# Strassen's seven products of quarters in place of eight, in the second product of an RWKV-6 plus SiLU kernel

**Chip, cores, metric.** One core of a Trainium2 chip. The metric is the device time of one execution in microseconds (us); lower is better.

## The reference

An attention block with a decayed state is followed by a two-layer feed-forward block over its output. Only the last part changes.

```python
# attention: r, k, v, w of shape (4 batches, 8 heads, 768 steps, 48); y has the same shape
for t in range(S):
    y[:, :, t] = r_t . (state + (u * k_t) v_t);  state = w_t * state + k_t v_t      # condensed
# feed-forward: x = y as (3072 tokens, 384)
h = x @ w_in                       # (3072, 384) @ (384, 2048)
g = h * (1.0 / (1.0 + np.exp(-h)))
out = g @ w_out                    # (3072, 2048) @ (2048, 384)  <- "the second product"
```

All arithmetic is fp32; w_in and w_out come as float64 and are rounded on the chip in the first 130 us.

## The kernel before

The 3072 tokens are taken in 12 units of 128 time steps x 2 batches. A unit's attention part (`mix`) has a serial chain of seven levels: TensorE makes score products (`p_sc`), VectorE copies them under a mask and multiplies r, and only then can the next level's products start. Between these steps the program puts independent feed-forward work of earlier units, so that TensorE always has something to do: the second product of the unit two back (`downs`), then the first product of the unit one back (`ups`).

```python
def up(i, m):                                     # first product, 2 of 16 feature blocks
    p_h = ps.tile([128, 2, TU], F32, name="p_h", bufs=2)
    # ... 6 matmuls of 256 columns ...
    nc.scalar.activation(out=gt[i, m], in_=p_h, func=AF.Silu)

def down(i, b, part, parts=4):                    # second product of batch b, 4 of 16 feature blocks
    if part == 0:
        po[i, b] = ps.tile([128, DM], F32, name="p_o", bufs=2)
    for f in range(part * FC // parts, (part + 1) * FC // parts):
        nc.tensor.matmul(po[i, b], lhsT=gt[i, f // 2][:, f % 2, b * L:(b + 1) * L], rhs=w_out_sb[:, f, :],
                         start=(f == 0), stop=(f == FC - 1))
    if part == parts - 1:
        ob = pt.tile([128, DM], F32, name="ob")
        nc.vector.tensor_copy(out=ob, in_=po[i, b])
        # ... store ...

def merge(*lists):                                # each list has shares; steps are ordered by their middle
    # ...
for i in range(3, NU):
    merge((mix(i), 0.0, 1.0), (downs(i - 2) + ups(i - 1), 0.0, 1.0))
merge((downs(NU - 2) + ups(NU - 1) + downs(NU - 1), 0.0, 1.0))
```

The order of steps is the order of each engine's queue. PSUM is the memory that TensorE's results land in, SBUF the one that holds the other tiles. Each tile in PSUM (`ps.tile`, at most 512 fp32 columns here) has a bank of its own; the program keeps eight of them (two each for `p_m`, `p_sc`, `p_h`, `p_o`).

## Time and profile before

| | before |
|---|---|
| time, median of the first 4 runs | 795.12 us (794.55 to 798.07) |
| TensorE busy | 93% of the span |
| units 5 to 11, level 0 to level 0 | 60.07 us |
| tail after the last attention step | 728.20 to 793.8 us |

First the engines' work in one unit, from one level 0 to the next (columns: stretch in us, its length, then per engine busy us and instructions):

```profile
core 0: us, PE busy (x) PEld busy (x) DVE busy (x) ACT busy (x) POOL busy (x), PEclk, DMA share, GB/s
259.02:319.09 60.07, 59.41 (x351) 45.25 (x351) 24.59 (x39) 9.64 (x20) 20.32 (x29) 1.00 0.33 52
```

TensorE (PE) has 0.66 us free out of 60.07. VectorE (DVE) works 24.59 us. Second, TensorE where the attention part of a unit ends (columns: start us, length us, engine, line, operation, out<-in, shapes, count, in brackets the idle time before and what ended it):

```profile
712.98 1.04 PE L368 MATMUL p_m<-ident,tk 128*128 128x128 f32 x8
714.30 1.13 PE L382 MATMUL p_m<-state,tr 128*128 128x96 f32 x8 [0.29 <-ACT kq L370]
```

L368 turns k back; L382 begins y of the first batch in the PSUM buffer that ScalarE (ACT) still has to empty. This is one of the few places where TensorE waits at all.

### The profile page before, as it was taken

The page shows a single profiled execution, that of the slowest core. Times are in us where ns is not written, and L with a number is a line of the kernel's source. Part 1 is how long each engine was busy: PE and PEld are TensorE (multiplying, and loading weights), DVE is VectorE, ACT ScalarE, POOL GpSimd, SP SyncE. Part 2 cuts the span into 40 slices and gives each one's busy share as a digit, 9 for nine tenths or more (in the row PEclk, how much of TensorE's full clock was granted, in tenths as well). Part 3 has the DMA queues.
Part 4 walks back from the last instruction along what each step waited for, and adds up shares of the span by engine and source line. Part 5 has one row for each costly group of instructions (what it writes and reads, how often), then busy time and mean ns, then how long its engine had stood idle before and what let it go on. Part 6 is the DMA issues. An engine that isn't in the chain of part 4 may idle for free.

```text
span 793.8 us, 11597 instructions
## 1 busy us (share of the span) xinstructions
PE 739.6 (93%) x4232; PEld 565.2 (71%) x4232; DVE 324.3 (41%) x489; ACT 161.8 (20%) x300; POOL 283.8 (36%) x398
## 2 busy tenths in 40 slices
PE   4486689999999999999999999999999999999998
PEld 3375577687688688688588588588588588588684
DVE  3675785431443443443443443443443442440000
ACT  3236345112121021021021021022012012021020
POOL 8555765521531531522522522522432431520000
PEclk9976799999999999999999999999999999999999
DMA  9986053022232522522522522422422120000000
GB/s 197 269 178 192 1 117 53 19 32 25 55 64 26 86 45 26 96 34 25 96 35 26 94 36 38 78 34 26 91 35 26 42 50 1 10 11 1 21 1 20
DMA packets 215880, 45.82 MB, mean 58 GB/s; under 512 B 207504, under 2 KB 210704, under 8 KB 215824
## 3 DMA queue, kind: packets, MB, share of 16 engines
q1 hardware_dynamic: 215680, 44.89, 30.4%
q8 instruction: 34, 0.56, 0.3%
q10 hardware_dynamic: 144, 0.20, 0.1%
q14 instruction: 22, 0.18, 0.1%
HBM read 40.30 MB, written 4.72 MB: 57 GB/s over the span
## 4 chain that ended last, share of the span: by engine, by line
PE 82%; POOL 6%; issue 5%; DVE 4%; ACT 2%; DVEq 0%; POOLq 0%
PE p_h L466 31%; PE p_o L476 29%; PE p_sc L331 11%; PE p_m L386 5%; PE p_m L382 3%; PE p_m L397 2%; POOL tk L362 2%; DVE tr L346 1%; DVE score L340 1%; POOL tw L293 1%; POOL w_in_sb L194 1%; ACT gt L469 1%; PE p_m L418 1%; PE p_m L277 1%; ACT kq L370 1%
## 5 line engine op out<-in xcount | busy, mean ns | idle before, releaser
L466 PE MATMUL p_h<-xt,w_in_sb 128*128 128x256 f32 x1152 | 272.6, 390 | 0.0
L476 PE MATMUL p_o<-w_out_sb,gt 128*128 128x384 f32 x768 | 258.6, 490 | 0.0
L466 PEld LDWEIGHTS p_h<-xt,w_in_sb 128*128 128x128 f32 x1152 | 216.6, 193 | 32.6 <-issue 0.2
L340 DVE COPY_PREDICATED score<-mask,p_sc 128x512 f32<-128x512 int8 x168 | 138.4, 888 | 221.5 <-PE p_sc L331 219.6
L476 PEld LDWEIGHTS p_o<-w_out_sb,gt 128*128 128x128 f32 x768 | 142.3, 190 | 93.6
L362 POOL TENSOR_TENSOR tk<-tk,tw 128x256 f32<-128x256 f32 x168 | 120.5, 741 | 124.0 <-PE p_sc L331 56.4
L331 PEld LDWEIGHTS p_sc<-tr,tk 48*128 48x128 f32 x1344 | 88.8, 199 | 69.7 <-issue 30.8
L331 PE MATMUL p_sc<-tr,tk 48*128 48x128 f32 x1344 | 105.3, 299 | 33.5 <-DVE tr L346 21.1
L469 ACT ACTIVATE gt<-p_h 128x512 f32<-128x512 f32 x96 | 57.3, 597 | 355.6 <-PE p_h L466 355.6
L322 ACT COPY tk<-tk 128x256 f32<-128x256 f32 x72 | 32.4, 450 | 178.3 <-POOL tk L362 133.1
L293 POOL TENSOR_TENSOR tw<-tw 128x512 f32<-128x512 f32 (+6 forms) x84 | 37.5, 446 | 86.8 <-DVE tw L268 65.1
L346 DVE TENSOR_TENSOR tr<-tr,tw 128x512 f32<-128x512 f32 x84 | 67.4, 803 | 0.0
L401 POOL TENSOR_TENSOR state<-state,tw 128x384 f32<-128x384 f32 x16 | 13.2, 826 | 120.1 <-PE p_m L382 120.1
L480 DVE COPY ob<-p_o 128x384 f32<-128x384 f32 x24 | 13.4, 556 | 96.8 <-PE p_o L476 96.8
L389 DVE TENSOR_TENSOR xb<-p_m,ydiag 128x384 f32<-128x384 f32 x24 | 13.4, 557 | 75.7 <-PE p_m L386 75.7
L308 POOL TENSOR_TENSOR ydiag<-vt,diag 128x384 f32<-128x384 f32 x24 | 19.9, 828 | 64.8 <-DVE diag L305 61.4
L407 DVE TENSOR_TENSOR state<-p_m,state 48x192 f32<-48x192 f32 x32 | 11.4, 355 | 48.2 <-PE p_m L397 48.0
L277 PE MATMUL p_m<-ident,raw 128*128 128x128 f32 x96 | 18.1, 338 | 12.7 <-DMA raw<-in_w_dram 5.9
L277 PEld LDWEIGHTS p_m<-ident,raw 128*128 128x128 f32 x96 | 14.0, 174 | 16.9 <-POOL mask L235 5.8
L301 POOL TENSOR_TENSOR ruk<-ruk,u_bc 128x384 f32<-128x384 f32 x24 | 24.0, 1000 | 1.9
L386 PE MATMUL p_m<-vq,score 128*128 128x48 f32 x192 | 24.6, 284 | 0.0
L382 PE MATMUL p_m<-state,tr 128*128 128x96 f32 x160 | 21.8, 279 | 2.9 <-ACT kq L370 2.9
(55 smaller groups left out, 437.2 us busy)
## 6 DMA issues: line engine op xcount, KB each, us to landing
vt<-in_v_dram SPq DMA_DIRECT2D x24, 192.0 KB, 3.7
out_dram<-ob SPq DMA_DIRECT2D x24, 192.0 KB, 1.9
w_out_sb<-in_moe_w_in_dram SPq DMA_DIRECT2D x5, 768.0 KB, 6.8
w_out_sb<-in_moe_w_out_dram SPq DMA_DIRECT2D x4, 768.0 KB, 5.2
own<-in_moe_w_out_dram SPq DMA_DIRECT2D x4, 768.0 KB, 4.7
own<-in_r_dram SPq DMA_DIRECT2D x16, 192.0 KB, 3.4
own<-in_k_dram SPq DMA_DIRECT2D x16, 192.0 KB, 3.5
vq<-in_v_dram SPq DMA_DIRECT2D x48, 48.0 KB, 2.6
```

The lines of the kernel that those rows point to most:

```text
L277: nc.tensor.transpose(p_tr[:, p, :], pair(raw[:, i % NSLOT, b, WRK[name]], p), ident)
L293: nc.gpsimd.tensor_tensor(out=up, in0=t[:, :, 0::2], in1=t[:, :, 1::2], op=ALU.mult)
L322: nc.scalar.copy(out=keys(next_at * L + c, [4 * c, NP * ni // 2], [c, 2], [1, c]), in_=keys(c, [4 * c, NP * ni // 2], [NP * L + c, 2], [1, ...
L331: nc.tensor.matmul(bass.AP(tensor=s_p.tensor, offset=s_p.offset, ap=[s_p.ap[0], [apart * L // 2, 2], [1, L // 2]]), lhsT=tk[i][rows, x_at ...
L340: nc.vector.copy_predicated(out=dst, mask=masks[l][:, :, None].to_broadcast([128, NB, NP, ni, c]), data=sc[e].rearrange("p (b q) (i c) -> ...
L346: nc.vector.tensor_tensor(out=rb[:, :, :, 1, :], in0=rb[:, :, :, 1, :], in1=t[:, :, 0::2][:, :, :, None].to_broadcast([128, Q, ni, c]), op ...
L362: nc.gpsimd.tensor_tensor(out=out, in0=have, in1=odd, op=ALU.mult)
L382: nc.tensor.matmul(p_y[:, 2 * p:2 * p + 2, :].rearrange("p a b -> p (a b)"), lhsT=tr[i][:, b * NP + p, :], rhs=state[:, b0 + b, p, :], sta ...
L386: nc.tensor.matmul(p_y[:, h, :], lhsT=score[:, i % NSC, h % 2, b * NP + h // 2, :], rhs=values(i, b)[:, h, :], start=(n == 0 and h == 0), ...
L466: nc.tensor.matmul(p_h[:, a, :], lhsT=w_in_sb[:, c, f * 128:(f + 1) * 128], rhs=xt[i][:, c, :], start=(c == 0), stop=(c == KC - 1))
L469: nc.scalar.activation(out=gt[i, m], in_=p_h, func=AF.Silu)
L476: nc.tensor.matmul(po[i, b], lhsT=gt[i, f // 2][:, f % 2, b * L:(b + 1) * L], rhs=w_out_sb[:, f, :], start=(f == 0), stop=(f == FC - 1))
```

## The change

The second product of two batches is a matrix of 2 batches x 2 feature halves times 2 feature halves x 2 output halves. Strassen's algorithm makes the four result quarters from seven quarter products instead of eight, at the price of sums: four sums of activations per pair of feature blocks, four sums of weight quarters (once), and sums of the results. The intent is an eighth less TensorE work in the second product. To make room in SBUF the buffers of v, of the bonus's r and k, and of the weight rounding's scratch are cut, and some loads are issued later.

```diff
-            vt[i, b] = pin.tile([128, H, D], F32, name="vt", bufs=3 * NB)
+            vt[i, b] = pin.tile([128, H, D], F32, name="vt", bufs=2 * NB)
 # ... vq 3 -> 2 buffers, ydiag 3 -> 2, r and k for the bonus in one buffer of their own,
 # ... v loaded one unit ahead instead of two, scratch "temps" shared by rounding and sums ...
+    NPLAIN = 1                                  # unit 0 keeps the plain product
+    def weight_sums(which):
+        out, one, two = ((t1, b12, b11), (t2, b22, t1), (t3, b22, b12), (b12, b21, t2))[which]
+        nc.vector.tensor_tensor(out=out, in0=one, in1=two, op=ALU.subtract)
+    def sums(i, m):
+        # ... s1 = lower1 + upper1, s2 = s1 - lower0, s3 = lower0 - lower1, s4 = upper0 - s2,
+        # ... four vector.tensor_tensor of 128x256
+    def quarter(i, which):
+        if which % 2 == 0:
+            po[i] = ps.tile([128, 2, DH], F32, name="p_o", bufs=2)
+        p = po[i][:, which % 2, :]
+        left, right = (...)[which]
+        for f in range(FH):
+            nc.tensor.matmul(p, lhsT=left(f), rhs=right[:, f, :], start=(f == 0), stop=(f == FH - 1))
+        # ... u1 to u4: tiles "partial"; c11 to c22: quarters of the output tiles "ob" ...
+        if which == 0:
+            nc.vector.tensor_copy(out=u1, in_=p)
+        for to, known in ((), ((u2, u1),), ((c11, u1),), ((u3, u2),), ((c22, u3), (u4, u2)), ((c21, u3),), ((c12, u4),))[which]:
+            nc.vector.tensor_tensor(out=to, in0=p, in1=known, op=ALU.add)
+        # ... store the output tiles after products 5 and 6 ...
     def ups(i):
+        # ... sums(i, 0), (i, 1), (i, 2) put behind up products 5, 6, 7
     def downs(i):
+        return [(0, sums, i, FH // 2 - 1)] + [(1, quarter, i, x) for x in range(7)]
```

More of the change, by code (lines that the diff above doesn't have):

```diff
@@ L99, in load_values @@
         for b in range(NB):
-            vt[i, b] = pin.tile([128, H, D], F32, name="vt", bufs=3 * NB)
+            vt[i, b] = pin.tile([128, H, D], F32, name="vt", bufs=2 * NB)
             nc.sync.dma_start(out=vt[i, b], in_=v[b0 + b, :, t0:t0 + L, :].rearrange("h t d -> t h d"))
-        vq[i] = pin.tile([128, H, D], F32, name="vq", bufs=3)
+        vq[i] = pin.tile([128, H, D], F32, name="vq", bufs=2)
         for g in range(4):
@@ L131 @@
     own = const.tile([128, NOWN, 2 * PW], U32, name="own")
+    tokens_rk = const.tile([128, NB, 2, H, D], F32, name="tokens_rk")
     def rk(i, b, x):
-        if i < NTOK:
-            return raw[:, i % NSLOT, b, 1 + x, :, 0:D]
-        return own[:, 1 + i % 2].bitcast(F32).rearrange("p (b x h d) -> p b x h d", b=NB, x=2, h=H)[:, b, x]
+        return raw[:, i % NSLOT, b, 1 + x, :, 0:D] if i < NTOK else tokens_rk[:, b, x]
     def staged(i):
@@ L163 @@
     half = {}
+    temps = const.tile([128, 3, 2, PW], U32, name="temps")
     def split_weight(i):
         hi = staged(i)[:, 1::2]
-        head = pt.tile([128, PW], U32, name="head")
+        head = temps[:, 0, i % 2]
         nc.vector.tensor_scalar(out=head, in0=hi, scalar1=0x7FFF0000, scalar2=None, op0=ALU.bitwise_and)
-        tail = pt.tile([128, PW], F32, name="tail")
+        tail = temps[:, 1, i % 2].bitcast(F32)
         nc.scalar.activation(out=tail, in_=staged(i).bitcast(U16)[:, 2::4], func=AF.Copy, scale=8.0)
@@ L177, in join_weight @@
         dst = w_ends[i][0].bitcast(U32)
-        low = pt.tile([128, PW], U32, name="low")
+        low = temps[:, 2, i % 2]
         def like(t):
@@ L185, in join_weight @@
                                        op0=ALU.bitwise_and, op1=ALU.bitwise_or)
-        sums.append((dst, like(head), like(low)))
-    sums = []
+        joined.append((dst, like(head), like(low)))
+    joined = []
     def add_weight():
-        while sums:
-            dst, head, low = sums.pop(0)
+        while joined:
+            dst, head, low = joined.pop(0)
             nc.gpsimd.tensor_tensor(out=dst, in0=head, in1=low, op=ALU.add)
@@ L306, in bonus_values @@
                                 axis=mybir.AxisListType.X, op=ALU.add)
-        ydiag[i, b] = pt.tile([128, H, D], F32, name="ydiag", bufs=3)
+        ydiag[i, b] = pt.tile([128, H, D], F32, name="ydiag", bufs=2)
         nc.gpsimd.tensor_tensor(out=ydiag[i, b], in0=vt[i, b], in1=diag.to_broadcast([128, H, D]), op=ALU.mult)
@@ L448, in mix @@
                 loads = [(0, load_blocks, i + NSLOT, name, b, g) for name in "wkr" for b in range(NB) for g in range(4)]
-            loads.append((0, load_values, i + NSLOT))
+        if 2 <= i + 1 < len(units):
+            loads.insert(len(loads) // 2, (0, load_values, i + 1))
         if NTOK <= i + 1 < len(units):
-            loads.insert(0, (0, load_rk, i + 1))
+            loads.insert(len(loads) // 4, (0, load_rk, i + 1))
         spread, room = steps[:last], len(steps) - last
@@ L478, in down @@
         if part == parts - 1:
-            ob = pt.tile([128, DM], F32, name="ob")
-            nc.vector.tensor_copy(out=ob, in_=po[i, b])
+            ob_b = pt.tile([128, DM], F32, name="ob")
+            nc.vector.tensor_copy(out=ob_b, in_=po[i, b])
             row0 = (b0 + b) * S + n * L
-            nc.sync.dma_start(out=out[row0:row0 + L, :], in_=ob)
-    def ups(i):
-        return [(1, up, i, m) for m in range(FC // 2)]
+            nc.sync.dma_start(out=out[row0:row0 + L, :], in_=ob_b)
@@ new lines @@
+    NPLAIN = 1
+    FH, DH = FC // 2, DM // 2
+    quarters = temps.rearrange("p a b e -> p (a b e)").bitcast(F32)[:, 0:4 * FH * L].rearrange("p (s f t) -> p s f t", s=4, f=FH)
+    b11, b12, b21, b22 = (w_out_sb[:, x * FH:(x + 1) * FH, y * DH:(y + 1) * DH] for x in range(2) for y in range(2))
+    t1, t2, t3 = (own[:, x].bitcast(F32).rearrange("p (f d) -> p f d", f=FH) for x in range(3))
+    def weight_sums(which):
+        out, one, two = ((t1, b12, b11), (t2, b22, t1), (t3, b22, b12), (b12, b21, t2))[which]
+        nc.vector.tensor_tensor(out=out, in0=one, in1=two, op=ALU.subtract)
@@ new lines, in sums @@
+    def sums(i, m):
+        lower, upper = (gt[i, x].rearrange("p a (b t) -> p b a t", b=NB) for x in (m, m + FH // 2))
+        s1, s2, s3, s4 = (quarters[:, x, 2 * m:2 * m + 2, :] for x in range(4))
+        for out, one, two, op in ((s1, lower[:, 1], upper[:, 1], ALU.add), (s2, s1, lower[:, 0], ALU.subtract),
+                                  (s3, lower[:, 0], lower[:, 1], ALU.subtract), (s4, upper[:, 0], s2, ALU.subtract)):
+            nc.vector.tensor_tensor(out=out, in0=one, in1=two, op=op)
@@ new lines, with g, s @@
+    ob = {}
+    def quarter(i, which):
+        n, b0 = units[i]
+        def g(b, half):
+            return lambda f: gt[i, (f + half * FH) // 2][:, f % 2, b * L:(b + 1) * L]
+        def s(x):
+            return lambda f: quarters[:, x, f, :]
+        if which % 2 == 0:
+            po[i] = ps.tile([128, 2, DH], F32, name="p_o", bufs=2)
+        p = po[i][:, which % 2, :]
+        left, right = ((g(0, 0), b11), (s(1), t2), (g(0, 1), b21), (s(2), t3), (s(0), t1), (g(1, 1), b12), (s(3), b22))[which]
+        for f in range(FH):
+            nc.tensor.matmul(p, lhsT=left(f), rhs=right[:, f, :], start=(f == 0), stop=(f == FH - 1))
+        if which == 0:
+            ob[i] = [pt.tile([128, DM], F32, name="ob") for b in range(NB)]
+            po[i, "u"] = pt.tile([128, 4, DH], F32, name="partial", bufs=1)
+        c11, c12, c21, c22 = (ob[i][x][:, y * DH:(y + 1) * DH] for x in range(2) for y in range(2))
+        u1, u2, u3, u4 = (po[i, "u"][:, x, :] for x in range(4))
+        if which == 0:
+            nc.vector.tensor_copy(out=u1, in_=p)
+        for to, known in ((), ((u2, u1),), ((c11, u1),), ((u3, u2),), ((c22, u3), (u4, u2)), ((c21, u3),), ((c12, u4),))[which]:
+            nc.vector.tensor_tensor(out=to, in0=p, in1=known, op=ALU.add)
+        if which >= 5:
+            b = 6 - which
+            row0 = (b0 + b) * S + n * L
+            nc.sync.dma_start(out=out[row0:row0 + L, :], in_=ob[i][b])
@@ L487, in downs @@
+    def ups(i):
+        steps = [(1, up, i, m) for m in range(FC // 2)]
+        if i >= NPLAIN:
+            for m in range(FH // 2 - 1):
+                steps.insert(FH // 2 + 2 + 2 * m, (0, sums, i, m))
+        return steps
     def downs(i):
-        return [(1, down, i, b, p) for b in range(NB) for p in range(4)]
+        if i < NPLAIN:
+            return [(1, down, i, b, p) for b in range(NB) for p in range(4)]
+        return [(0, sums, i, FH // 2 - 1)] + [(1, quarter, i, x) for x in range(7)]
@@ L505 @@
           (weights[:3], 0.2, 0.75), (weights[3:10], 0.78, 1.2), (weights[10:13], 1.2, 1.75), (weights[13:], 1.78, 2.2),
-          (ups(0), 1.0, 2.0), (ups(1)[:2], 2.0, 2.125), (downs(0), 2.125, 2.625), (ups(1)[2:], 2.625, 3.0))
+          (ups(0), 1.0, 2.0), (ups(1)[:2], 2.0, 2.125), (downs(0), 2.125, 2.625), (ups(1)[2:], 2.625, 3.0),
+          ([(1, weight_sums, x) for x in range(3)], 2.3, 2.6), ([(1, weight_sums, 3)], 2.7, 2.8))
     for i in range(3, NU):
```

## The prediction

> **What bounds the kernel now.** I read the page first (busy shares, the chain that ended last), then the groups, then the timeline of one unit. A unit is one of the 12 steps of 2 batches x 128 tokens.
>
> ```profile
> PE 739.6 (93%) x4232; PEld 565.2 (71%) x4232; DVE 324.3 (41%) x489; ACT 161.8 (20%) x300; POOL 283.8 (36%) x398
> ...
> PE 82%; POOL 6%; issue 5%; DVE 4%; ACT 2%; DVEq 0%; POOLq 0%
> ...
> L466 PE MATMUL p_h<-xt,w_in_sb 128*128 128x256 f32 x1152 | 272.6, 390 | 0.0
> L476 PE MATMUL p_o<-w_out_sb,gt 128*128 128x384 f32 x768 | 258.6, 490 | 0.0
> ```
>
> TensorE is 93% busy, and 82% of the last-ending chain is TensorE. The second product (p_o) is a third of its work, so an eighth of that is worth having. There are 12 x 2 x 16 = 384 products in the source and 768 records: each f32 product leaves two. The means (390, 490 ns) overlap and are no rate; the rate is start to start, which the tail of the timeline gives:
>
> ```profile
> 741.74 7.26 PE L476 MATMUL p_o<-w_out_sb,gt 128*128 128x384 f32 x22
> 748.84 20.88 PE L466 MATMUL p_h<-xt,w_in_sb 128*128 128x256 f32 x96
> 769.56 20.80 PE L476 MATMUL p_o<-w_out_sb,gt 128*128 128x384 f32 x64
> ```
>
> The first group is cut by the window but starts on a record: (748.84 - 741.74)/22 = 322.7 ns per record of 384 columns; (769.56 - 748.84)/96 = 215.8 ns at 256 columns. The line through both is 0.835 ns a column plus about 2 ns.
>
> How the attention part of a unit stands among the feed-forward products decides what the change is worth. TensorE and VectorE from one unit, levels 0 to 3:
>
> ```profile
> 677.73 1.18 PE L331 MATMUL p_sc<-tr,tk 48*128 48x128 f32 x16
> 678.84 5.43 PE L476 MATMUL p_o<-w_out_sb,gt 128*128 128x384 f32 x16
> 684.20 1.18 PE L331 MATMUL p_sc<-tr,tk 48*128 48x128 f32 x16
> 685.31 2.85 PE L476 MATMUL p_o<-w_out_sb,gt 128*128 128x384 f32 x8
> 688.51 1.16 PE L331 MATMUL p_sc<-tr,tk 48*128 48x128 f32 x16 [0.36 <-DVE tr L346]
> ```
> ```profile
> 678.95 2.49 DVE L340 COPY_PREDICATED score<-mask,p_sc 128x512 f32<-128x512 int8 x2 [10.04 <-PE p_sc L331]
> 681.24 0.72 DVE L346 TENSOR_TENSOR tr<-tr,tw 128x512 f32<-128x512 f32 x1
> 681.89 0.53 DVE L480 COPY ob<-p_o 128x384 f32<-128x384 f32 x1
> 685.41 2.44 DVE L340 COPY_PREDICATED score<-mask,p_sc 128x512 f32<-128x512 int8 x2 [2.99 <-PE p_sc L331]
> 687.65 0.72 DVE L346 TENSOR_TENSOR tr<-tr,tw 128x512 f32<-128x512 f32 x1
> ```
>
> At levels 0 and 1 VectorE needs 4.2 us from the start of the score products to the end of its multiply (677.73 to 681.96; 684.20 to 688.37). TensorE covers that with feed-forward products: two pieces of eight records after level 0, no stall; one piece after level 1, and level 2 starts 0.4 us late. Otherwise TensorE waits for almost nothing; level 0 recurs every 60.07 us (259.02, 319.09, ... 619.42). VectorE has 24.6 us of work in such a unit (windows of 59 us), so it isn't a bound by throughput, but its queue is in order, which matters below.
>
> **What the Trainium skill says.** (1) "TensorE: Matmul & The Clock Gate", Back-to-back issue gap: N/2.4 + 2.5 ns a pass warm; LDWEIGHTS is P/1.2, 107 ns for 128 columns whatever the moving side. "FP8 and Floating Point Precision", TensorE Precision Notes, gives true FP32 four passes. Two records of two passes make 2N/2.4 + 2.5: 322.5 at 384, 215.8 at 256, as the trace has it. The weight load's floor shows too: 16 records of only 48 columns took 717.02 - 715.27 = 1.75 us, 109 ns each. (2) "VectorE: DVE Perf Modes", the TRN2 errata: an fp32 tensor_tensor takes (N + 151)/0.96 ns. The trace: 557 ns at 384 (formula 557), 355 at 192 (357), 0.67 to 0.68 us at 512 in a quiet place (691). (3) "PSUM — Partial Sum Buffer", PSUM bank collisions: TensorE may not write a bank while another engine reads it in the same partitions, even at other columns; "Semaphore-guard PSUM by bank × quadrant". The old kernel shows no such case, as each output tile is one group read once at its end. The new one makes one.
>
> **The change part by part.**
>
> *TensorE work.* Per unit before: 32 products of 384 columns, 64 records x 322.5 = 20.64 us. After: 7 x 8 = 56 products of 192 columns, 112 records x (2 x 192/2.4 + 2.5 = 162.5 ns) = 18.20 us. Well above the 109 ns of a weight load, so loads stay hidden. Saved 2.44 us a unit, and 11 of 12 units are done so: 26.8 us, all on the bound engine.
>
> *VectorE work.* Sums of quarters: 16 tensor_tensor of 256 columns a unit, (256+151)/0.96 = 424 ns, 6.8 us. Outputs: 8 reads of 192 columns at 357 ns (2.86 us) for 2 of 556 (1.11). Together +8.5 us a unit, 24.6 to 33 us of some 59: still half idle. Four sums of weights (1536 columns, 1.76 us each, 7 us) once, in the third unit.
>
> *New waits.* Two quarter products now share one output tile (half a bank each). By (3) the second of a pair (products 1, 3, 5) can't start before VectorE has read the first. I worked out the merged order of steps from the source for a unit from the fifth on: product 0, product 1, product 2, level 0, product 3, level 1, product 4, product 5, level 2, product 6, level 3.
> - 0 to 1: nothing of TensorE between (those units transpose on VectorE). VectorE starts a read about 0.11 us after TensorE could have gone on, 0.36 us for the read, 0.14 us from VectorE's end to TensorE's start (688.37 to 688.51): 0.61 us. VectorE has two blocks of sums and a transpose ahead of it there, late by an estimated 0.1: 0.7 us.
> - 2 to 3: level 0 (1.1 us of TensorE) lies between; hidden.
> - 4 to 5: VectorE reads product 4 only after level 1's multiply, which ends 4.17 us after level 1 starts. Two reads (c22, u4), 0.65 us; plus 0.14: product 5 starts 4.9 us after level 1, when TensorE was done at 1.11 + 2.60 = 3.71. Stall 1.2 us.
> - Level 0 now has one piece behind it (0.4 us late) and level 1 two: as before, exchanged.
> - After the back-transposes of k there is now an up product before y, which hides the ScalarE copy that y waited for (712.98 + 0.86 to 714.30, 0.46 us); y of the second batch then waits some 0.14. Net -0.3.
>
> *Sum.* A unit from the fifth on: -2.44 + 0.7 + 1.2 - 0.3 = -0.84 us; eight of them, -6.7. The fourth unit still transposes on TensorE, which covers pair 0/1, and product 2 covers the 1.12 us that level 0 waited there for ScalarE: -2.44 + 1.2 - 0.3 - 1.1 + 0.4 (a wait for a transpose buffer) = -2.2. Tail, two second products with nothing between: 2 x (-2.44 + 0.61 + 0.61 + 0.9) and a last read shorter by 0.2 us: -0.8. Weight sums in front of two levels: +0.4. Total -9.3, so 795.3 - 9.3 = 786.
>
> *Moved loads.* v arrives one unit ahead instead of two, r and k for the bonus into one buffer instead of two. Both are issued in the middle of the unit before, tens of us early, against 3.5 us to land: nothing. In the first 130 us loads change places, but the weight rounding on VectorE and POOL sets that pace; estimated +-1 us.
>
> **The rivals.**
> *A: the bank isn't guarded as a whole; the pairs overlap freely.* Then the 0.7 and 1.2 (and 2.1 in each tail unit) go: 9 x 1.2 + 8 x 0.7 + 4.2 = 20.6 us more, 765. For it: the columns are disjoint. Against: point (3), and a kernel that ignored it would fault.
> *B: the pairs are guarded, and VectorE's queue costs more still:* sums written in order after one another wait for each other, a read of an output holds back the transposes and keeps behind it, and level 1 or GpSimd's products slip. About 0.6 us a unit more eats the gain: 791 to 797. For it: reads of products 0, 1 and 2 stand between the transposes. Against: from my order these end about 1 us before level 0 needs them.
> *C: records of 192 columns are no cheaper than a weight load lets them be.* Had each cost 185 ns, 112 records would take 20.7 us, no gain at all, and with the waits 813. For it: weight-load records last 190 ns each. Against: those overlap; 16 in a row ran at 109 ns apiece.
>
> **Range and chances.** My sum gives 1.2%. The gain in TensorE work is sure to a few tenths of a us; the stalls are inferred, and each of the two is multiplied by eight or more. Half of them missing makes 776, B's delays 795: 775 to 796. Faster by over 2% means below 779.4: I give it 0.24, within 2% 0.72, slower 0.04.
>
> **What would show it.** Right: p_o records 162 to 163 ns apart start to start; TensorE idle some 0.6 us in front of product 1 and 1.2 us in front of product 5, released by VectorE's read of p_o, and nothing in front of 3; level 0 recurring every 59.2 us instead of 60.07; VectorE 33 us a unit. The prediction is wrong if product 5 starts straight behind product 4 (A), if the records stand wider than 170 ns (C), or if level 0 or GpSimd's products start late behind VectorE (B).

## The result

| | before | after |
|---|---|---|
| median of 4 runs | 795.12 us | 784.01 us |
| range | 794.55 to 798.07 | 783.3 to 786.56 |
| ratio | | 0.9859 (95%: 0.9826 to 0.9892) |
| level 0 to level 0 | 60.07 us | 59.00 us |

Ratios here are the mean time of one kernel's runs over that of the other's of the same rounds, so not quite the ratio of the medians quoted. The change gains 1.4%, inside the 2% that counts as the same, though clear of noise. Lines of the changed kernel's page that answer to those of before:

```profile
PE 718.5 (92%) x4760; PEld 634.9 (81%) x4760; DVE 410.3 (52%) x735; ACT 163.4 (21%) x300; POOL 288.0 (37%) x398
...
PE 61%; SPq 14%; DVE 13%; issue 6%; POOL 5%; DMA 1%; ACT 1%; DVEq 0%; POOLq 0%
...
L524 PE MATMUL p_o<-w_out_sb,gt 128*128 128x192 f32 x528 | 92.4, 328 | 8.4 <-DVE partial L533 8.4
L524 PE MATMUL p_o<-own,temps 128*128 128x192 f32 x528 | 94.0, 332 | 6.2 <-DVE partial L531 5.3
```

TensorE is busy 21 us less but the span fell only by 12. VectorE's share rose from 41% to 52% and it now stands in the chain with 13% instead of 4%. The last two lines say where: TensorE sat idle in front of second-product matmuls until VectorE had read a partial result, a wait the kernel before didn't have. (SPq, the DMA queue, has 14% of the chain too. That is a trap of following a chain: where a load lands just before its use, the chain goes through the load. In the stretches concerned the one VectorE instruction that waited for a load did so for 0.18 us, at 611.24, and the units from 197.57 to 610.60 took 59.00 to 59.02 us, no more than the others.)

The timeline of TensorE in one unit, from product 0 over the levels 0 and 1 to product 5:

```profile
306.85 2.77 PE L524 MATMUL p_o<-w_out_sb,gt 128*128 128x192 f32 x16
310.18 2.87 PE L524 MATMUL p_o<-own,temps 128*128 128x192 f32 x16 [0.57 <-DVE partial L531]
312.89 2.76 PE L524 MATMUL p_o<-w_out_sb,gt 128*128 128x192 f32 x16
315.58 1.18 PE L331 MATMUL p_sc<-tr,tk 48*128 48x128 f32 x16
316.69 2.87 PE L524 MATMUL p_o<-own,temps 128*128 128x192 f32 x16
319.96 1.18 PE L331 MATMUL p_sc<-tr,tk 48*128 48x128 f32 x16 [0.40 <-DVE tr L346]
321.06 2.87 PE L524 MATMUL p_o<-own,temps 128*128 128x192 f32 x16
324.71 2.87 PE L524 MATMUL p_o<-w_out_sb,gt 128*128 128x192 f32 x16 [0.78 <-DVE partial L533]
```

Products 0 to 5 are the six L524 lines. The waits in brackets stand in front of 1 and 5, not in front of 2, 3 or 4. VectorE at the same places (other engines' lines left out):

```profile
309.04 0.70 DVE L268 STREAM_TRANSPOSE tw<-raw 128x512 f32<-128x512 f32 x1
309.77 0.36 DVE L531 COPY partial<-p_o 128x192 f32<-128x192 f32 x1
...
321.14 2.47 DVE L340 COPY_PREDICATED score<-mask,p_sc 128x512 f32<-128x512 int8 x2 [1.07 <-PE p_sc L331]
...
323.42 0.71 DVE L346 TENSOR_TENSOR tr<-tr,tw 128x512 f32<-128x512 f32 x1
324.05 0.34 DVE L533 TENSOR_TENSOR ob<-p_o,partial 128x192 f32<-128x192 f32 x1
324.31 0.34 DVE L533 TENSOR_TENSOR partial<-p_o,partial 128x192 f32<-128x192 f32 x1
```

The read of product 0 ends at 310.13 and product 1 starts at 310.18. The two reads of product 4 come only after level 1's copies and multiply, end at 324.65, and product 5 starts at 324.71, though product 4's last matmul had left TensorE free a microsecond before.

### The profile page after: what moved, and what is told of

Same layout as the page of the kernel before. It is cut to its first block, busy times and chain, and to the rows that moved or that the text cites. A ratio compares the mean times of both kernels' runs of the same rounds, so it can differ in the third digit from the quotient of the medians.

```text
span 781.6 us, 12898 instructions
## 1 busy us (share of the span) xinstructions
PE 718.5 (92%) x4760; PEld 634.9 (81%) x4760; DVE 410.3 (52%) x735; ACT 163.4 (21%) x300; POOL 288.0 (37%) x398
## 4 chain that ended last, share of the span: by engine, by line
PE 61%; SPq 14%; DVE 13%; issue 6%; POOL 5%; DMA 1%; ACT 1%; DVEq 0%; POOLq 0%
PE p_h L467 22%; PE p_o L524 17%; SPq L93 12%; PE p_sc L331 10%; DVE score L340 5%; PE p_m L386 4%; PE p_o L477 2%; DVE tr L346 2%; DVE temps L504 2%; PE p_m L397 2%; PE p_m L382 1%; SPq L106 1%; POOL tw L293 1%; POOL w_in_sb L194 1%; PE p_m L368 1%
## 5 line engine op out<-in xcount | busy, mean ns | idle before, releaser
L524 PE MATMUL p_o<-w_out_sb,gt 128*128 128x192 f32 x528 | 92.4, 328 | 8.4 <-DVE partial L533 8.4
L524 PE MATMUL p_o<-own,temps 128*128 128x192 f32 x528 | 94.0, 332 | 6.2 <-DVE partial L531 5.3
L524 PEld LDWEIGHTS p_o<-w_out_sb,gt 128*128 128x128 f32 x528 | 85.6, 190 | 11.7 <-DVE partial L533 11.7
L524 PEld LDWEIGHTS p_o<-own,temps 128*128 128x128 f32 x528 | 85.0, 190 | 12.0 <-DVE partial L531 8.3
L346 DVE TENSOR_TENSOR tr<-tr,tw 128x512 f32<-128x512 f32 x84 | 63.7, 759 | 0.0
L533 DVE TENSOR_TENSOR ob<-p_o,partial 128x192 f32<-128x192 f32 x44 | 15.6, 355 | 63.8 <-PE p_o L524 63.8
L504 DVE TENSOR_TENSOR temps<-gt 128x256 f32<-128x256 f32 x88 | 37.0, 420 | 21.8 <-ACT gt L470 21.5
L524 PE MATMUL p_o<-w_out_sb,temps 128*128 128x192 f32 x176 | 31.3, 332 | 0.0
L524 PEld LDWEIGHTS p_o<-w_out_sb,temps 128*128 128x128 f32 x176 | 28.4, 190 | 1.1
```

What stands on the lines that cost most here:

```text
L346: nc.vector.tensor_tensor(out=rb[:, :, :, 1, :], in0=rb[:, :, :, 1, :], in1=t[:, :, 0::2][:, :, :, None].to_broadcast([128, Q, ni, c]), op ...
L504: nc.vector.tensor_tensor(out=out, in0=one, in1=two, op=op)
L524: nc.tensor.matmul(p, lhsT=left(f), rhs=right[:, f, :], start=(f == 0), stop=(f == FH - 1))
```

## The experiments

Nine runs of eight kernels, in three groups, each with its runs of the kernel before (median 794.9 to 795.4 us; the second group takes over those of the first). All outputs are right.

**Own banks for all products.** Each quarter product gets an output tile of its own.

```diff
-        if which % 2 == 0:
-            po[i] = ps.tile([128, 2, DH], F32, name="p_o", bufs=2)
-        p = po[i][:, which % 2, :]
+        po[i] = ps.tile([128, DH], F32, name="p_o", bufs=2)
+        p = po[i]
```

> Each quarter product gets an output tile of its own (a bank of its own, two in rotation) instead of half of one. Theory (two products of a pair may not overlap because they share a bank): the stalls in front of products 1 and 5 go (0.84 and 1.1 us a unit), those in front of 1, 3 and 5 in the two tail units too (2.4 us each): 784.0 - 8 x 1.94 - 1.1 - 4.8 = 762.6 us, 4.1% below the kernel before. Rival (the stalls come from VectorE's queue being late with its reads, whatever bank they are in): the stalls move behind other products or in front of the attention levels, and the time stays between 778 and 784.

Measured: 764.17 us, ratio to before 0.9611 (0.9589 to 0.9633). TensorE at the same places:

```profile
307.20 2.77 PE L523 MATMUL p_o<-w_out_sb,gt 128*128 128x192 f32 x16
309.81 2.76 PE L523 MATMUL p_o<-own,temps 128*128 128x192 f32 x16
...
320.58 2.87 PE L523 MATMUL p_o<-own,temps 128*128 128x192 f32 x16
323.28 2.76 PE L523 MATMUL p_o<-w_out_sb,gt 128*128 128x192 f32 x16
```

Product 1 follows product 0 after 2.61 us (it was 3.33), product 5 follows 4 after 2.70 (it was 3.65), and nothing is idle in between. VectorE's instructions are the same and in the same order; only the bank is different. The unit takes 57.12 us instead of 59.00. So the shared bank made the waits, and the rival, that VectorE's late reads would cost as much from any bank, is refuted. In these kernels a tile in PSUM is also a bank, and the waits are for semaphores, which the program sets; so no run tells whether the guard goes by the bank or by the tile, or what would come of leaving it out. This version beats both kernels. Run again, it was expected as follows.

> Own banks alone, in the same rounds, to set beside the reordered one: 764 us, as before, and a unit of 57.12 us in the trace.

Measured: 764.6 us, ratio 0.9606 (0.9581 to 0.963); the unit took 57.13 to 57.15 us.

**Own bank for product 5 alone.**

```diff
-        if which % 2 == 0:
+        if which % 2 == 0 or which == 5:
             po[i] = ps.tile([128, 2, DH], F32, name="p_o", bufs=2)
-        p = po[i][:, which % 2, :]
+        p = po[i][:, 0 if which == 5 else which % 2, :]
```

> Only product 5 gets an output tile of its own; pairs 0/1 and 2/3 still share. Theory: 1.1 us in each of nine units and 0.8 in each of the two tail units go: 784.0 - 9.9 - 1.6 = 772.5 us, and the 0.57 us idle in front of product 1 stays. Rival as for the run with own banks: nothing or under 4 us gained, level 2 starts no earlier.

Measured: 772.28 us, ratio 0.9726 (0.9705 to 0.9746). In the trace product 1 still waits 0.56 us, and product 5 follows product 4 after 2.70 us. A little over half of what own banks bring comes from this one pair, as the two stalls' sizes have it.

**Everything but the seven products.**

```diff
-    NPLAIN = 1
+    NPLAIN = 12
-          ([(1, weight_sums, x) for x in range(3)], 2.3, 2.6), ([(1, weight_sums, 3)], 2.7, 2.8))
```

> The changed kernel with the second product as before in all units and no sums: what is left are the moved loads, the smaller buffers and the shared scratch memory. Theory: they cost nothing; the first 187 us were 0.7 us shorter in the changed kernel's trace, so 794 to 796 us. Rival: the moved loads carry part of the gain (the last 600 us gain as well), under 792 us.

Measured: 796.36 us, ratio 1.0016 (0.9992 to 1.004): the same as before. Units take 60.06 us. The moved loads and smaller buffers neither cost nor gain anything that these runs can show.

**The kernel before, with one up product in front of y.** The program's order is made with one exchange.

```diff
 # ... for each neighbouring pair of the order, up to the first that fits ...
+            if order[x][0] is y and order[x + 1][0] is up and order[x][2] == 0 and len(lists) == 2:
+                order[x], order[x + 1] = order[x + 1], order[x]
```

> The kernel before, with one exchange in units 4 to 12: the up product that stands behind y of the first batch goes in front of it. Theory (in the changed kernel one step fewer in the list moved this product forward, which hides the wait for ScalarE's copy, and 0.53 us a unit of the gain come from that and not from the seven products): 795.1 - 9 x 0.5 = 790.5 us. Rival (the gain there is from something else, such as the earlier read of k): 794 to 796 us.

Measured: 791.43 us, ratio 0.9956 (0.9934 to 0.9978). The unit took 59.53 us (level 0 at 260.58 and 320.11) against 60.07: 0.54 us from an exchange of two steps in the old kernel, without any Strassen. The changed kernel has that order, and no wait in front of y (L382), which the view at 714.30 above showed:

```profile
290.40 1.04 PE L368 MATMUL p_m<-ident,tk 128*128 128x128 f32 x8
291.28 2.75 PE L467 MATMUL p_h<-xt,w_in_sb 128*128 128x256 f32 x12
293.87 1.03 PE L382 MATMUL p_m<-state,tr 128*128 128x96 f32 x8
```

**The changed kernel, with that product put back behind y.** The same exchange the other way round.

```diff
 # ... for each neighbouring pair of the order, up to the first that fits ...
+            if order[x][0] is up and order[x + 1][0] is y and order[x + 1][2] == 0 and len(lists) == 2:
+                order[x], order[x + 1] = order[x + 1], order[x]
```

> The changed kernel with one exchange: in units 4 to 12 the up product goes back behind y of the first batch, as the kernel before has it. Theory: the 0.5 us wait in front of y returns, nothing else moves: 784.0 + 9 x 0.5 = 788.5 us. Rival (the run that moved it in the kernel before gained by chance): 783 to 785.5 us.

Measured: 788.19 us, ratio 0.9912 (0.9895 to 0.9929); the unit takes 59.53 us instead of 59.00. Both directions agree: some 4 of the 11 us that the change gained come from this side effect. With 15 steps of feed-forward work in place of 16, the merged order moved by one place there.

**The sums of quarters worked out twice.**

```diff
-            nc.vector.tensor_tensor(out=out, in0=one, in1=two, op=op)
+            for _ in range(2):
+                nc.vector.tensor_tensor(out=out, in0=one, in1=two, op=op)
```

> Every sum of quarters is worked out twice (the second time gives the same values), 6 us more of VectorE work in a unit, which still leaves it a third idle. Theory (VectorE's queue stands on the path at the start of a unit, where three blocks of sums lie ahead of the read that product 1 waits for): that read comes some 4.3 us later in each of eight units, 784 + 35 = 819 us, all of it in front of product 1. Rival (idle VectorE time absorbs the sums): under 787 us.

Measured: 859.67 us, ratio 1.0824 (1.08 to 1.0847). The direction was right, the size wrong by a factor of two: 75.7 us, not 35. TensorE, and then VectorE, in a unit of this run:

```profile
322.42 2.77 PE L525 MATMUL p_o<-w_out_sb,gt 128*128 128x192 f32 x16
...
330.86 0.36 DVE L532 COPY partial<-p_o 128x192 f32<-128x192 f32 x1
...
331.27 4.30 PE L525 MATMUL p_o<-own,temps 128*128 128x192 f32 x16 [6.09 <-DVE partial L532]
```

Product 1 starts 8.85 us after product 0 instead of 3.33, 5.5 us more: a doubled block of sums took 3.31 us (320.20 to 323.51) against 1.47, so 1.84 us more and not 1.45, three times (each repeat writes what the instruction before it wrote, and 1.84 / 4 = 0.46 us is also what lies between a sum and the next one that reads it, against 0.34 us between independent ones). And product 1 itself takes 4.13 us until the next one starts at 335.40, where it took 2.71. The stretches of idle time and of product 1 by themselves (the PEclk column, after the busy times, is the granted clock):

```profile
325.02:331.27 6.25, 0.17 (x2) 0.00 (x0) 5.98 (x16) 0.00 (x0) 0.00 (x0) 0.69 0.21 25
331.27:335.40 4.13, 4.13 (x16) 4.13 (x17) 1.75 (x3) 1.42 (x3) 3.01 (x7) 0.64 0.22 27
335.40:338.10 2.70, 2.70 (x19) 2.48 (x17) 1.66 (x3) 0.00 (x0) 0.00 (x0) 1.00 0.23 26
```

The clock fell to a mean of 0.64 while product 1 ran and was back at 1.00 for product 2. This unit (level 0 at 272.13 and 338.10) took 65.97 us against 59.00: 5.5 of idle time and 1.4 of slow clock. The Trainium skill, "TensorE: Matmul & The Clock Gate", Part 1, says that an idle window of some 3.4 us puts the clock back to half; this trace agrees, with 6.09 us of idleness, and the idle times of 0.57 and 0.78 us in the changed kernel left it at 1.00. Other units took 67.1 us, alternating with these. The extra 1.1 us is more of the same: in the next unit product 1 took 5.27 us (397.22 to 402.49) at a granted clock of 0.50, against 4.13 at 0.64. Of the 76 us between the two traces 58.6 lie in the eight units from 197.57 (205.10 here) on, 7.5 before them and 10.0 after them; the expectation counted the eight units alone, and without the slow clock. What the run settles: VectorE, half idle by its busy share, stands on the path at the start of a unit, and work put there is paid in full.

**Own banks and a new order.** The up products run in the pairs that the sums need, so that the sums spread out; VectorE's transposes all go ahead of its first read of an output; two quarter products stand behind level 0 and two behind level 1.

```diff
 # ... own banks as above ...
+            steps = [(1, up, i, m + a) for m in range(FH // 2) for a in (0, FH // 2)]
-                steps.insert(FH // 2 + 2 + 2 * m, (0, sums, i, m))
+                steps.insert(3 + 3 * m, (0, sums, i, m))
-            steps += [(1, turn, i, b, name) for b in range(NB)]
+            steps += [(1 if i < NTOK else 0.15, turn, i, b, name) for b in range(NB)]
-            steps.append((LEVEL, level, i, l))
+            steps.append((LEVEL if i < NTOK else (5, 4.4, 2.6, 2.6, 2.6, 2.6, 2.6)[l], level, i, l))
```

> Own banks, and a new order: up products run in the pairs that the sums need (0, 4, 1, 5 ...), so that the sums spread over the levels; VectorE's transposes all stand ahead of its first read of an output; two quarter products stand behind level 0 and two behind level 1. Theory (with the banks parted, the wait of 0.4 us in front of level 1 is the last one left in a unit from the fifth on): 764.2 - 8 x 0.4 = 761 us. Rival (VectorE's reads now come later than the buffers allow, two in rotation): 764 us or more.

Measured: 762.59 us, ratio 0.9598 (0.9578 to 0.9618), not to be told from own banks alone; a miss. The unit took 57.08 us against 57.12. The wait in front of level 1 is gone as meant, and another has taken its place at level 0:

```profile
309.17 1.18 PE L331 MATMUL p_sc<-tr,tk 48*128 48x128 f32 x16 [0.42 <-DVE tr L268]
```

L268 are VectorE's transposes: in front of them in its queue the unit's last block of sums waited 1.17 us for ScalarE. So the wait moved up the same queue, as neither theory had it.

**Own banks, the new order, and that block between the transposes.**

```diff
-            steps += [(1 if i < NTOK else 0.15, turn, i, b, name) for b in range(NB)]
+            steps += [(1 if i < NTOK else 0 if name == "w" else 0.2, turn, i, b, name) for b in range(NB)]
```

> The reordered kernel again, with one change: its trace shows the last block of sums of a unit waiting 1.2 us for ScalarE at the start of the next and holding the transposes back, so that level 0 starts 0.42 us late. Here two transposes go in front of that block and four behind it. Theory (level 0 was held by the transposes alone): level 0 loses its wait in eight units, level 1 keeps none, 762.6 - 8 x 0.4 = 759.3 us, 4.5% below the kernel before. Rival (the next thing in VectorE's queue, its first reads of outputs behind the shuffle of v, takes over): 761.5 to 763 us.

Measured: 762.84 us, ratio 0.9587 (0.9568 to 0.9606), against 0.9606 for own banks in the same rounds: not to be told apart, a second miss. The time lies in the rival's range, but not by its cause: level 0 still waits for a transpose (L268), now 0.58 us. The block no longer waits for ScalarE, but it runs slower (VectorE, then GpSimd (POOL), in the same stretch):

```profile
304.60 0.43 DVE L504 TENSOR_TENSOR temps<-gt 128x256 f32<-128x256 f32 x1
305.06 1.14 DVE L504 TENSOR_TENSOR temps<-temps,gt 128x256 f32<-128x256 f32 x1
306.13 0.83 DVE L504 TENSOR_TENSOR temps<-gt 128x256 f32<-128x256 f32 x1
```
```profile
304.72 3.83 POOL L293 TENSOR_TENSOR tw<-tw 128x512 f32<-128x512 f32 x7 [8.07 <-DVE tw L268]
```

The two transposes that I moved forward release GpSimd's products of w, which run during the sums: the sums take 1.14 and 0.83 us instead of 0.42, GpSimd's seven products 3.83 instead of 3.48. The Trainium skill, "SBUF — State Buffer", Who interferes with whom, says that a VectorE instruction with two SBUF inputs contends with a GpSimd instruction that reads SBUF; these lines fit it, though no run here takes the GpSimd work away to prove it. Neither order beats plain own banks by more than the runs can show.

## Why the prediction was right

I predicted 786.0 us, 775 to 796; the kernel took 784.01. In the terms of its sum, read off the two traces:

| step | predicted, us | measured, us | read from |
|---|---|---|---|
| record of 192 columns | 0.1625 | 0.1625 | last product before the tail's ups: (736.83 - 734.23)/16 |
| products 0 to 1, per unit | +0.7 | +0.84 | 312.89 - 306.85, less 2 x 2.60 |
| products 4 to 5, per unit | +1.2 | +1.05 | 324.71 - 321.06 - 2.60; against own banks 3.65 - 2.70, and 0.10 more in product 5 |
| y after the back-transposes, per unit | -0.3 | -0.53 | 251.19 - 234.21 before, 306.85 - 290.40 after |
| whole unit from the fifth on | -0.84 | -1.07 | 60.07 to 59.00 |
| fourth unit | -2.2 | -2.6 | 63.44 to 60.82 |
| tail | -0.8 | -0.2 | 65.60 to 65.39 |
| start, up to the fourth unit | +0.4 | -0.7 | 187.75 to 187.03 |

With the 2.44 us of TensorE work saved, the terms of a unit add up to -2.44 + 0.84 + 1.05 - 0.53 = -1.08 us, for the -1.07 measured.

- *The TensorE work.* Right, though the working has a slip: with 2.5 ns a pass, as it says, a record of two passes would have 5; the rates of the trace (215.8 and 322.7 ns, and 162.5 now) have room for one 2.5 only, as its formula has it. Own banks show it bare: the tail's second product takes 721.66 - 703.46 = 18.20 us, the predicted figure, for the 20.6 of before. Rival C (records held at the weight load's pace) is refuted by the 162.5 ns.
- *The waits at the shared bank.* Right in mechanism, place and releaser: in front of 1 and 5, none in front of 3 where level 0 lies between. Rival A (the pairs overlap freely) is refuted by the trace, and own banks turn it into a kernel: 764.2 us, where the rival had said 765. So some 20 of the 26.8 us of saved TensorE work went into these waits.
- *The size of the waits.* Two terms were off in opposite directions. From VectorE's end to TensorE's start I took 0.14 us from a score product; here it is 0.05 to 0.06; and product 4's two reads end 0.52 us after the multiply, where I took 0.65 (the sum 4.17 + 0.65 + 0.14 is 4.96, which I gave as 4.9; measured 324.71 - 319.96 = 4.75). On the other side, the first product after a stall needs about 0.1 us more than one in a stream (2.70 or 2.71 for 2.60), which I had left out: its first weight load starts with it (both at 310.18), where in a stream it starts 0.16 us ahead (312.73 for 312.89), which fits a load of about 0.1 us that is no longer hidden, though no run tests it. In the tail three such pieces make 2.42 us of loss for each second product (20.62 - 18.20), not 2.12.
- *y.* The step was right, the size half: I set off 0.14 us of new waiting for the second batch's y, and the trace has 0.07 of it; y's first product, no longer behind a wait, also takes 0.87 us where it took 0.96.
- *VectorE.* 31.6 us in a unit (windows from 256.58 to 374.58), where I said 33. Its queue was late with product 0's read by 0.21 us, twice the estimated 0.1: the read could have begun at about 309.56 and began at 309.77, behind the sums and a transpose. Rival B (VectorE's queue costs more still) did not happen at these loads; doubling the sums shows how near it was.
- *Moved loads.* Nothing, as said: the run with everything but the products is the same as before. The start's -0.7 is one trace against another; traces of the same kernel differ by 3 us there (the fourth unit's level 0 at 200.85 and 197.64 in the two profiles with own banks), for a reason that I did not find. So the differences of the two traces, 12.2 us, and of the medians, 11.1, are as close as they can be asked to be, and how near the sum of 9.3 came to them is in part chance: 1.1 us of the gap to the traces lies in the start, where the +0.4 for the sums of weights is below what the runs can show.

## What to carry to other kernels

Before counting a smaller matmul bill as time, look at where its results land: two products that share a PSUM bank ran one after the other's read here, wherever too little other work of TensorE stood between them; that took back three quarters of the saving, and a bank each removed it. An engine that is half idle can still be on the path wherever its queue, in order, stands between two products of the busy one. And an edit that removes a step from a merged order shifts all the others; measure that shift by itself, since here it made a third of the gain and was to be had without the change.

## What the Trainium skill lacked or had wrong

- "TensorE: Matmul & The Clock Gate": no spacing for fp32 products. An fp32 product shows as two records, and each takes 2N/2.4 + 2.5 ns: 162.5 at 192 columns, 215.8 at 256, 322.5 at 384.
- The same page: nothing on the first product after a stall. 16 records took 2.70 us after one, 2.60 in a stream.
- "PSUM — Partial Sum Buffer": it tells to guard a bank, not what the guard costs: between products of 192 columns in the same bank 0.61 to 0.73 us beyond the product's own 2.60, with one read between them and VectorE free or nearly so, and 1.05 us with two reads and VectorE late.
- "SBUF — State Buffer": no size for this pair of instructions. Sums of 256 columns took 0.62 to 1.14 us beside GpSimd products, 0.42 alone (as said, no run proves that the products are the cause).
- "VectorE: DVE Perf Modes": no size for dependence. A sum of 256 columns started 0.46 us after one whose result it reads or writes again, 0.34 us after an independent one; no page has the difference.
